# A stored order of steps, ScalarE's factors in registers and one fp32 head pair fewer, in attention followed by a gated MLP

## The chip, the core and the metric

The kernel runs on one core of a Trainium2 chip. The metric is the device time of one execution in microseconds, taken from the median of several runs. Five engines work side by side, each through its own instruction stream in order: TensorE (PE; PEld is its weight load), VectorE (DVE), ScalarE (ACT), GpSimd (POOL, nearly unused here) and SyncE (SP), which issues the DMAs. Engines wait for one another by semaphores.

## The reference

Attention with soft-capped scores over 4 batches of 12 heads (448 positions, 64 wide), then two matrix products with a gate between them:

```python
scores = cap * np.tanh(scale * np.matmul(q, k.transpose(0, 1, 3, 2)) / cap)
scores = scores - np.max(scores, axis=-1, keepdims=True)
attn = np.exp(scores)
attn = attn / (np.sum(attn, axis=-1, keepdims=True) + 1e-09)
x = np.matmul(attn, v)      # (4, 12, 448, 64), then laid out as (1792, 768)
h = x @ w_in                # 768 -> 2048
g = h * (1.0 / (1.0 + np.exp(-1.702 * h)))
out = g @ w_out             # 2048 -> 768
```

The two weights arrive as 64-bit floats.

## The kernel before

**Units.** Attention is cut into 24 units, one for each pair of heads: 6 pairs in each of 4 batches, in that order. Unit u makes the scores of its pair transposed (keys on the partitions) in four groups (`GROUPS`, three of two 448-column banks and one of one bank), and each group goes PE (tile `s`), Tanh on ACT (`t`), Exp on ACT, and then back to PE twice: `sm` sums the exponentials with a matrix of ones, `pa` multiplies them by v. DVE multiplies `pa` with the reciprocal of the sums (`rb`), which takes a way through four small DMAs (`sd`, `rsum`, `rd`, `rb`).

**Two kinds of unit.** The first `F32_UNITS` units (8 before) feed PE with fp32 operands, straight from the DMA: `kk`, `qh` and `vd` or space in `wo`. All later units are split: each fp32 tensor becomes a high and a low 16-bit float (`kk` with both halves stacked, `qh` and `ql`, `vh` and `vl`, `p` with two planes), and PE makes the products from those. For that a split unit needs one instruction that rounds each tensor, on ACT or DVE (`scaled`), and one that subtracts, on DVE (`stt`, `tt`).

**The MLP.** Batches 0 and 1 go through `h_unit` (6 x 3 matmuls into `m` for each of 16 rows of h) and `o_unit` (16 x 3 for each of 6 rows of the output). Batches 2 and 3 go together, by a seven-product scheme: `moe_sums` prepares sums of weight blocks, `x_last` sums of activations, `h_quad` makes eight sets of seven products into six banks `z`, and `seven_first` and `seven` the output. DVE decodes the 64-bit weights into two 16-bit halves (`decode_w`) in the meantime.

**PE's tile forms.** PE holds matmuls of five forms (rows x columns of the array): 128x128 for the MLP and the scores of split units, 64x128 and 64x64 for fp32 scores, 128x64 for `pa`, 128x32 for `sm`. I call a step from a matmul of one form to one of another a switch.

**The order.** Nothing runs when it is recorded. `Plan.op` keeps each step with its engines (some steps may go to ACT or DVE, `scaled`), its duration by a table and what it depends on. `schedule` then runs a list scheduler: 30 passes of `forward` (the step that can start first goes next, ties by priority) and `backward` (new priorities from the latest starts), keeps the best pass, and `refine` moves runs of PE steps of one form next to runs of the same form if that makes the modelled total shorter. Buffers of a ring get their slots in passing. `emit` writes the steps out in that order.

**ACT's factors.** Tanh takes its scale from `tsc`, Exp its scale from `capt` and, in split units, its bias from `lnb`: three 128x1 tiles, one number for each partition, read by every such instruction.

Of the kernel before, what the change touches and what calls it, by code (L numbers as in the profile page):

```python
# [9 lines left out]
F32 = mybir.dt.float32  # L10
# [13 lines left out]
F32_UNITS = 8  # L24
# [11 lines left out]
PASSES = 30  # L36
# [15 lines left out]
PE_TURN = 0.093  # L52
# [5 lines left out]
DVE_SHY = (1.0,)  # L58
STAY = (0.0,)
ROUNDS, RUN, REACH = 4, 6, 20.0  # L60
# [48 lines left out]
class Plan:  # L109
# [118 lines left out]
    def start_over(self):  # L228
        bufs = {b for o in self.ops for b in o.bufs}
        for b in bufs:  # L230
            b.left, b.freed = 0, 0.0
            if b.ring:
                b.slot = None
        for o in self.ops:
            o.left, o.ready = len(o.deps), 0.0
            o.eng = next(iter(o.ways)) if len(o.ways) == 1 else None
            for b in o.bufs:
                b.left += 1
        for r in self.rings:
            r["free"] = [(0.0, i) for i in range(len(r["tiles"]))]  # L240
            r["queue"] = list(r["turns"])

    def forward(self, shy, stay=0.0):

        self.start_over()
        free = {"PE": 0.0, "ACT": ACT_FROM, "DVE": ACT_FROM, "SP": 0.0}
        cand = {e: [o for o in self.ops if e in o.ways and not o.left] for e in free}
        turn, pipe = None, 0.0
        order = []
        while len(order) < len(self.ops):  # L250
            best = None
            for e, c in cand.items():
                for o in c:
                    t = max(o.ready + (shy if e == "DVE" and len(o.ways) > 1 else 0.0), free[e])
                    for b in o.bufs:
                        if b.slot is None:
                            r = b.ring
                            t = max(t, r["free"][0][0]) if r["free"] and (r["any"] or r["queue"][0] is b) else math.inf
                    k = (t, o.prio + (stay if e == "PE" and o.turn != turn else 0.0), o.ways[e][0])
                    if best is None or k < best[0]:  # L260
                        best = (k, e, o)
            assert best is not None and best[0][0] < math.inf, "no step can go on"
            (t, _, us), e, o = best
            for w in o.ways:
                cand[w].remove(o)
            o.eng, o.emit = e, o.ways[e][1]
            for b in o.bufs:
                if b.slot is None:
                    b.ring["queue"].remove(b)
                    b.slot = b.ring["free"].pop(0)[1]  # L270
            if e == "PE":
                us += PE_TURN * (o.turn != turn)
                turn = o.turn
            o.start, o.end = t, t + us
            free[e] = t + us
            done = t + us + LAG[e]
            if e == "SP":
                pipe = max(pipe, t + us) + o.mb / DMA_BW
                done = pipe + LAG[e]
            order.append(o)  # L280
            for u in o.users:
                u.left -= 1
                u.ready = max(u.ready, t + us if u.eng == e == "PE" else done + HANDOFF)
                if not u.left:
                    for w in u.ways:
                        cand[w].append(u)
            for b in o.bufs:
                b.left -= 1
                b.freed = max(b.freed, done + HANDOFF)
                if not b.left and b.ring:  # L290
                    b.ring["free"].append((b.freed, b.slot))
                    b.ring["free"].sort()
        return order

    def backward(self, order):

        after = {o: [(u, 0.0 if u.eng == o.eng == "PE" else LAG[o.eng] + HANDOFF) for u in o.users] for o in order}
        turns = {}
        for o in order:
            for b in o.bufs:  # L300
                if b.ring:
                    x = turns.setdefault((id(b.ring), b.slot), [])
                    if not x or x[-1][0] is not b:
                        x.append((b, []))
                    x[-1][1].append(o)
        for x in turns.values():
            for (_, was), (_, then) in zip(x, x[1:]):
                for o in was:
                    after[o].append((then[0], LAG[o.eng] + HANDOFF))
        before = {o: [] for o in order}  # L310
        for o, xs in after.items():
            for u, lag in xs:
                before[u].append((o, lag))
        left = {o: len(xs) for o, xs in after.items()}
        end = max(o.end for o in order)
        due = {o: end for o in order}
        free = dict.fromkeys(("PE", "ACT", "DVE", "SP"), end)
        cand = [o for o in order if not left[o]]
        start = {}
        while cand:  # L320
            o = max(cand, key=lambda o: (min(due[o], free[o.eng]), o.end))
            cand.remove(o)
            free[o.eng] = start[o] = min(due[o], free[o.eng]) - (o.end - o.start)
            for q, lag in before[o]:
                due[q] = min(due[q], start[o] - lag)
                left[q] -= 1
                if not left[q]:
                    cand.append(q)
        return start

    def schedule(self):

        best = None
        for i in range(PASSES):
            stay = STAY[i % len(STAY)] if i else 0.0
            order = self.forward(DVE_SHY[0], stay)
            total = max(o.end for o in order)
            if best is None or total < best[0]:
                best = (total, stay, {o: o.prio for o in order})
            for o, t in self.backward(order).items():  # L340
                o.prio = t
        for o, p in best[2].items():
            o.prio = p
        self.order = self.forward(DVE_SHY[0], best[1])
        self.refine(ROUNDS)
# [21 lines left out]
    def timed(self, pre, seqs, limit=math.inf):  # L367
# [5 lines left out]
        turn, pipe, left = None, 0.0, n  # L373
        while left:
            moved = False
            for e, s in seqs.items():
                k = at[e]
                while k < len(s):
                    i = s[k]
                    t = free[e]  # L380
                    for p, near in pre[i]:
                        if start[p] is None:
                            t = None
                            break
                        x = end[p] if near else done[p] + HANDOFF
                        if x > t:
                            t = x
                    if t is None:
                        break
                    o = self.order[i]  # L390
                    us = o.ways[e][0]
# [4 lines left out]
                    free[e] = t + us  # L396
                    if e == "SP":
                        pipe = max(pipe, t + us) + o.mb / DMA_BW
                        done[i] = pipe + LAG[e]
                    else:  # L400
                        done[i] = t + us + LAG[e]
                    if end[i] > limit:
                        return None
                    k += 1
                    left -= 1
                    moved = True
                at[e] = k
            if not moved:
                return None
        return start, end, max(end)  # L410

    def refine(self, rounds):

        pre = self.edges()
        seqs = {e: [i for i, o in enumerate(self.order) if o.eng == e] for e in ("PE", "ACT", "DVE", "SP")}
        start, end, best = self.timed(pre, seqs)
        for _ in range(rounds):
            gained = False
            k = 1
            while k < len(seqs["PE"]):  # L420
                s = seqs["PE"]
                turn = lambda j: self.order[s[j]].turn
                if turn(k) == turn(k - 1):
                    k += 1
                    continue
# [1130 lines left out]
```

## Time and profile before

| | |
|---|---|
| Time, median of 3 runs | 603.84 us (603.43 to 603.88) |
| The profiled execution | 603.16 us |
| Its span, first to last instruction | 600.9 us |
| Granted TensorE clock, mean | 0.998 |
| PE busy | 589.3 us, 98% of the span, 3666 matmuls |
| PE's weight loads busy | 281.5 us, 47% |
| DVE busy | 540.5 us, 90%, 898 instructions |
| ACT busy | 414.2 us, 69%, 610 instructions |
| DMA | 73.87 MB, 123 GB/s over the span |
| Chain that ended last | PE 86%, DVE 5%, DMA 4%, ACT 2% |

The span is the time between the first and the last instruction on the core; 2.26 us of the profiled execution lie outside it. Busy times are unions of an engine's instructions, so two that overlap by a little count once. The helper functions record every operation, so nearly all instructions carry one of a few line numbers (L218 is every matmul, L183 most of DVE, L175 and L199 most of ACT), and tile names tell them apart.

### The profile page before, as it was taken

The page shows a single profiled execution, that of the slowest core. Times are in us where ns is not written, and L with a number is a line of the kernel's source. Part 1 is how long each engine was busy: PE and PEld are TensorE (multiplying, and loading weights), DVE is VectorE, ACT ScalarE, POOL GpSimd, SP SyncE. Part 2 cuts the span into 40 slices and gives each one's busy share as a digit, 9 for nine tenths or more (in the row PEclk, how much of TensorE's full clock was granted, in tenths as well). Part 3 has the DMA queues.
Part 4 walks back from the last instruction along what each step waited for, and adds up shares of the span by engine and source line. Part 5 has one row for each costly group of instructions (what it writes and reads, how often), then busy time and mean ns, then how long its engine had stood idle before and what let it go on. Part 6 is the DMA issues. An engine that isn't in the chain of part 4 may idle for free.

```text
span 600.9 us, 9852 instructions
## 1 busy us (share of the span) xinstructions
PE 589.3 (98%) x3666; PEld 281.5 (47%) x3666; DVE 540.5 (90%) x898; ACT 414.2 (69%) x610; POOL 0.2 (0%) x4
## 2 busy tenths in 40 slices
PE   7999999999999999999999999999999999999995
PEld 3332344444544444445554445455555555555552
DVE  4999999999999999999999989878999999968912
ACT  5998896999987987999879779834555554211100
POOL 0000000000000000000000000000000000000000
PEclk9999999999999999999999999999999999999999
DMA  8988864226567443513343453022222210001001
GB/s 297 383 234 246 296 220 149 81 53 208 154 193 231 157 130 87 178 46 109 109 122 130 127 174 120 30 83 58 71 76 65 53 54 1 31 15 47 32 15 50
DMA packets 45556, 73.87 MB, mean 123 GB/s; under 512 B 14952, under 2 KB 31168, under 8 KB 45504
## 3 DMA queue, kind: packets, MB, share of 16 engines
q1 hardware_dynamic: 45504, 73.20, 38.4%
q8 instruction: 30, 0.49, 0.3%
q14 instruction: 22, 0.18, 0.1%
HBM read 61.22 MB, written 11.95 MB: 122 GB/s over the span
## 4 chain that ended last, share of the span: by engine, by line
PE 86%; DVE 5%; DMA 4%; ACT 2%; issue 1%; SPq 1%; DVEq 0%; ACTq 0%
PE m L218 43%; PE z L218 22%; PE s L218 9%; PE pa L218 9%; PE sm L218 3%; DMA wo<-in_moe_w_in_dram 1%; DMA rd<-rr 1%; ACT t L175 1%; SPq L224 1%; DVE ta L183 1%; DMA stg<-in_kx_dram 1%; DVE p L183 1%; ACT p L175 1%; DMA wo<-in_q_dram 1%; DVE f L183 0%
## 5 line engine op out<-in xcount | busy, mean ns | idle before, releaser
L218 PE MATMUL m<-g,wo 128*128 128x448 f16 x624 | 127.4, 353 | 0.0
L218 PEld LDWEIGHTS <-wo 128*128 128x128 f16 x864 | 81.8, 98 | 82.0 <-issue 9.0
L175 ACT ACTIVATE t<-s,tsc 128x896 f32<-128x896 f32 x96 | 86.8, 918 | 17.4 <-PE s L218 13.7
L218 PEld LDWEIGHTS <-wi_h 128*128 128x128 f16 x528 | 49.4, 98 | 56.2 <-issue 12.2
L218 PE MATMUL m<-x,wi_h 128*128 128x448 f16 x234 | 63.6, 353 | 0.0
L175 ACT ACTIVATE t<-t,lnb,capt 128x896 f32<-128x896 f32 (+1 forms) x58 | 59.4, 1030 | 0.4
L183 DVE TENSOR_TENSOR p<-t,p 128x896 f16<-128x896 f32 (+1 forms) x58 | 55.2, 954 | 4.1 <-ACT p L199 3.7
L218 PE MATMUL m<-xa,wi_h 128*128 128x448 f16 x198 | 53.7, 353 | 0.0
L218 PE MATMUL s<-qh,kk 128*128 128x448 f16 (+3 forms) x160 | 48.1, 403 | 0.0
L199 ACT ACTIVATE p<-t 128x896 f16<-128x896 f32 (+1 forms) x54 | 45.1, 838 | 0.3
L183 DVE SCALAR_TENSOR_TENSOR wo<-wo 128x1024 int32<-128x1024 int32 (+2 forms) x42 | 43.8, 1064 | 0.0
L218 PE MATMUL m<-x,wi_l 128*128 128x448 f16 x117 | 41.2, 352 | 0.0
L218 PEld LDWEIGHTS <-stg 128*128 128x128 f16 x288 | 28.2, 98 | 26.3
L218 PE MATMUL s<-ql,kk 128*128 128x448 f16 (+1 forms) x128 | 39.6, 352 | 0.0
L218 PEld LDWEIGHTS <-wi_l 128*128 128x128 f16 x264 | 25.8, 98 | 24.1
L199 ACT ACTIVATE xa<-x 128x1024 f16<-128x1024 f32 x9 | 9.5, 1057 | 38.3 <-PE z L218 27.3
L218 PE MATMUL pa<-p,vh 128*64 128x448 f16 x256 | 35.6, 356 | 0.4 <-DVE rb L183 0.4
L218 PE MATMUL m<-xa,wi_l 128*128 128x448 f16 x99 | 34.9, 352 | 0.0
L218 PEld LDWEIGHTS <-kk 128*128 128x128 f16 (+1 forms) x256 | 20.8, 100 | 23.4 <-issue 6.8
L218 PE MATMUL sm<-p,ones 128*32 128x224 f16 (+2 forms) x544 | 30.8, 313 | 0.5 <-ACT p L175 0.5
L218 PEld LDWEIGHTS <-xa 128*128 128x128 f16 x216 | 21.1, 98 | 19.6
L175 ACT ACTIVATE p<-t,capt 128x896 f32<-128x896 f32 (+1 forms) x32 | 29.6, 970 | 0.0
(282 smaller groups left out, 1078.4 us busy)
## 6 DMA issues: line engine op xcount, KB each, us to landing
wo<-in_moe_w_in_dram SPq DMA_DIRECT2D x18, 512.0 KB
stg<-in_kx_dram SPq DMA_DIRECT2D x16, 448.0 KB
stg<-in_qx_dram SPq DMA_DIRECT2D x16, 448.0 KB
stg<-in_moe_w_out_dram SPq DMA_DIRECT2D x16, 384.0 KB
wo<-in_moe_w_out_dram SPq DMA_DIRECT2D x16, 384.0 KB
sum<-xa SPq DMA_DIRECT2D x32, 192.0 KB
stg<-sum SPq DMA_DIRECT2D x32, 192.0 KB
rb<-rd SPq DMA_DIRECT2D x44, 112.0 KB
```

The source lines that it names most:

```text
L175: self.nc.scalar.activation(real(out), real(in_), func, scale=real(scale), **b)
L183: getattr(self.nc.vector, name)(out=real(out), **{k: real(x) for k, x in ins.items()}, **kw, **a)
L199: self.nc.scalar.activation(real(out), real(in_), AF.Copy, scale=1.0 if f is None else f, **b)
L218: self.nc.tensor.matmul(real(o), real(w), real(x), start=a, stop=z)
L224: self.nc.sync.dma_start(real(o), real(i))
```

## The change

There are three edits.

1. `F32_UNITS` is 7 instead of 8: unit 7 (batch 1, second pair) becomes a split unit.
2. `tsc` (two tiles) and `capt` are loaded into registers of ScalarE once, at the start (`held`, a register load on ACT), and Tanh and Exp name the register as their scale; Exp's bias is the constant log(64) in the instruction, and `lnb` is gone. None of these instructions reads a 128x1 tile any more. Since the planner's price of an ACT instruction depends on the number of such tiles, it now counts Tanh and Exp as cheaper.
3. The list scheduler (`start_over`, `forward`, `backward`, `refine`) is gone. `ORDER` is a compressed string: one 16-bit number for each step (the step's number, and one bit for which of its engines takes it), then one byte for each use of a ring for the slot. `schedule` reads it, and `timed` only gives the steps their places for `emit`.

```diff
-F32_UNITS = 8
+F32_UNITS = 7
...
+ORDER = (
+    "c-p;p1F+{!vSpSMzqW1Lwr$(C-F^SKecQHe+qP}nHeY`;`(|f1Uc`%;c)L|~PE}-NMpd1tjHpxqU_gTf1Of;7z2p!LQiBI6AUX)7fou>LQbGjC1u-Bkq=J}`6e2=)U`PiAy-1K7VnG?m0g)jORDjqJ1<FDk$O{!A"
...
     def schedule(self):
 
-        best = None
-        for i in range(PASSES):
...
-        self.order = self.forward(DVE_SHY[0], best[1])
-        self.refine(ROUNDS)
+        n = len(self.ops)
+        raw = zlib.decompress(base64.b85decode(ORDER))
+        slots = iter(raw[2 * n:])
         for r in self.rings:
+            for b in r["turns"]:
+                b.slot = next(slots)
+        self.order = []
+        for x in struct.unpack(f"<{n}H", raw[:2 * n]):
+            o = self.ops[x & 0x7FFF]
+            o.eng = list(o.ways)[x >> 15]
+            o.emit = o.ways[o.eng][1]
+            self.order.append(o)
...
+    def held(t):
+        r = nc.scalar.alloc_register()
+        nc.scalar.reg_load(r, t[:1].bitcast(I32))
+        return r
...
-        tsc.append(plan.fixed(t))
-    capt, lnb = plan.fixed(capt), plan.fixed(lnb)
+        tsc.append(held(t))
+    capt = held(capt)
...
-                plan.act(e[:, :nn], t[:, :nn], AF.Exp, scale=capt, bias=lnb)
+                plan.act(e[:, :nn], t[:, :nn], AF.Exp, scale=capt, bias=math.log(PS))
```

Counted over the whole order, PE switches its form 186 times before and 100 times now (the last check's one matmul left out); of these 80 and 52 have an fp32 matmul on one side.

PE, first fp32 units, from the first `pa` on (`s` are scores, `pa` products with v, `sm` sums; two instructions of one matmul count as x2). Before:

```order
L218 MATMUL pa_156<-p_134,wo 64x448 x2
L218 MATMUL sm_155<-p_134,ones_2_75 32x224 x4
L218 MATMUL sm_155<-p_135,ones_2_75 32x224 x4
L218 MATMUL s_160<-wo 128x448 x2
L218 MATMUL pa_156<-p_135,wo 64x448 x2
L218 MATMUL pa_156<-p_136,wo 64x448 x2
L218 MATMUL sm_155<-p_136,ones_2_75 32x224 x4
L218 MATMUL sm_155<-p_137,ones_0_73 32x224 x2
L218 MATMUL sm_155<-p_137,ones_1_74 32x224 x2
L218 MATMUL pa_156<-p_137,wo 64x448 x2
```

and now, in the same place:

```order
L257 MATMUL pa_161<-p_139,wo 64x448 x2
L257 MATMUL sm_160<-p_139,ones_2_74 32x224 x4
L257 MATMUL sm_160<-p_140,ones_2_74 32x224 x4
L257 MATMUL s_165<-wo 128x448 x2
L257 MATMUL s_166<-wo 128x448 x2
L257 MATMUL sm_160<-p_141,ones_2_74 32x224 x4
L257 MATMUL sm_160<-p_142,ones_0_72 32x224 x2
L257 MATMUL sm_160<-p_142,ones_1_73 32x224 x2
L257 MATMUL s_165<-wo 128x448 x2
L257 MATMUL s_166<-wo 64x448 x2
L257 MATMUL pa_161<-p_140,wo 64x448 x2
L257 MATMUL pa_161<-p_141,wo 64x448 x2
```

The three later `pa` of the first unit, which stood in two places, now stand together behind its sums, and scores of the next unit are drawn ahead of them.

ACT, its first steps after the table load (`t` is Tanh's output, `p` Exp's). Before:

```order
L529 ACTIVATE warm<-lnb 128x1
L175 ACTIVATE t_131<-s_160,tsc_111 128x896
L175 ACTIVATE t_132<-s_161,tsc_111 128x896
L175 ACTIVATE p_134<-t_131,capt 128x896
L175 ACTIVATE p_135<-t_132,capt 128x896
```

and now:

```order
L412 ACTIVATE warm<-warm 128x1
L432 TENSOR_LOAD tsc_110
L214 ACTIVATE t_136<-s_165 128x896
L214 ACTIVATE t_137<-s_166 128x896
L432 TENSOR_LOAD capt
L214 ACTIVATE p_139<-t_136 128x896
L214 ACTIVATE p_140<-t_137 128x896
```

One register load now stands ahead of the first Tanh, another between the second Tanh and the first Exp; the third stands ahead of the first split unit's Tanh.

SP, its first DMAs (`g` and `wo` are room for weight pieces, keys, queries and v that wait to be used). Before:

```order
L524 DMA capt<-in_cap_dram 128x1
L224 DMA wo<-in_k_dram 128x448
L224 DMA wo<-in_q_dram 128x448
L224 DMA wo<-in_v_dram 128x512
L224 DMA wo<-in_k_dram 128x448
L224 DMA wo<-in_q_dram 128x448
L224 DMA g<-in_moe_w_in_dram 128x1024 x4
```

and now:

```order
L408 DMA capt<-in_cap_dram 128x1
L263 DMA wo<-in_q_dram 128x448
L263 DMA wo<-in_k_dram 128x448
L263 DMA g<-in_moe_w_in_dram 128x1024 x2
L263 DMA wo<-in_v_dram 128x512
L263 DMA wo<-in_k_dram 128x448
L263 DMA wo<-in_q_dram 128x448
```

Two weight pieces moved ahead of v and of the second unit's keys and queries.

## Rows read from the trace of the kernel before

**Rows 1.** The page's part 1: busy time, share of the span, instructions.

```profile
PE 589.3 (98%) x3666; PEld 281.5 (47%) x3666; DVE 540.5 (90%) x898; ACT 414.2 (69%) x610; POOL 0.2 (0%) x4
```

**Rows 2.** Windows of the span: length, then busy us of each engine, clock, DMA.

```profile
0.00:20.00 20.00, 16.37 (x100) 6.65 (x100) 10.84 (x37) 13.98 (x18) 0.20 (x4) 1.00 0.89 328
...
200.00:280.00 80.00, 79.79 (x506) 39.22 (x504) 79.08 (x126) 69.20 (x99) 0.00 (x0) 1.00 0.39 120
...
340.00:400.00 60.00, 60.00 (x445) 28.73 (x443) 49.68 (x87) 44.97 (x67) 0.00 (x0) 1.00 0.36 113
400.00:520.00 120.00, 120.00 (x638) 62.00 (x635) 117.52 (x209) 60.61 (x108) 0.00 (x0) 1.00 0.17 51
```

**Rows 3.** Chain that ended last, in order of time: start us, us, what.

```profile
205.17 1.14 PE m L218 x6
206.82 2.39 PE pa L218 x24
209.21 1.24 PE m L218 x6
```

**Rows 4.** PE's instructions in time, fp32 units: start, us, operation, idle before.

```profile
28.23 0.97 PE L218 MATMUL pa<-p,wo 128*64 128x448 f32 x4
29.13 0.96 PE L218 MATMUL sm<-p,ones 128*32 128x224 f32 x16
30.03 1.77 PE L218 MATMUL s<-wo 64*128 64x448 f32 x8
31.73 0.96 PE L218 MATMUL sm<-p,ones 128*32 128x224 f32 x16
32.63 1.72 PE L218 MATMUL pa<-p,wo 128*64 128x448 f32 x8
34.28 1.92 PE L218 MATMUL s<-wo 64*64 64x448 f32 x8
```

**Rows 5.** The same at 16-bit forms.

```profile
205.00 1.30 PE L218 MATMUL m<-g,wo 128*128 128x448 f16 x6
206.23 0.59 PE L218 MATMUL sm<-ta,ones 128*32 128x224 f32 x8
```

**Rows 6.** The same, where PE waited.

```profile
5.15 4.08 PE L218 MATMUL s<-wo 64*128 64x448 f32 x12 [1.37 <-DMA wo<-in_q_dram]
9.58 0.97 PE L218 MATMUL s<-wo 64*64 64x448 f32 x4 [0.35 <-ACT t L175]
...
43.03 1.02 PE L218 MATMUL s<-wo 64*128 64x448 f32 x4 [0.80 <-ACT t L175]
...
276.66 0.57 PE L218 MATMUL pa<-p,vh 128*64 128x448 f16 x4 [0.21 <-DVE rb L183]
```

**Rows 7.** Groups by form, ACT: count, busy us, mean ns, idle before.

```profile
L175 ACT ACTIVATE f<-m 128x448 f32<-128x448 f32 x32 | 17.2, 541 | 3.3 <-PE m L218 3.3
L175 ACT ACTIVATE t<-s,tsc 128x448 f32<-128x448 f32 x24 | 15.3, 638 | 1.3 <-PE s L218 1.0 <-DVE ta L183 0.3
L175 ACT ACTIVATE t<-t,lnb,capt 128x448 f32<-128x448 f32 x16 | 12.2, 761 | 0.1
L175 ACT ACTIVATE stg<-stg 128x448 f32<-128x448 f32 x6 | 3.4, 575 | 2.6 <-DVE stg L183 2.6
```

**Rows 8.** DVE's instructions in time.

```profile
9.23 0.43 DVE L183 TENSOR_SCALAR g<-g 128x512 int32<-128x512 int32 x1 [5.00 <-DMA g<-in_moe_w_in_dram]
...
385.95 0.62 DVE L183 TENSOR_TENSOR rb<-x,rb 128x448 f32<-128x448 f16 x1
386.49 0.62 DVE L183 SCALAR_TENSOR_TENSOR xa<-ta,xa 128x448 f16<-128x448 f32 x1
...
595.30 0.13 DVE L1383 TENSOR_SCALAR flag<-cnt 1x1 int32<-1x1 f32 x1
```

**Rows 9.** SP's DMA issues in time.

```profile
2.14 0.43 SPq L224 DMA_DIRECT2D wo<-in_v_dram  x1
...
3.56 2.06 SPq L224 DMA_DIRECT2D g<-in_moe_w_in_dram  x4
```

More of the change, by code (lines that the diff above doesn't have):

```diff
@@ L1 @@
+import base64
 import math
+import struct
+import zlib
 from contextlib import ExitStack
@@ L243, in forward @@
[L243 to L250, printed above, removed]
-            best = None
[L252 to L329, printed above, removed]
@@ L331, in schedule @@
-    def schedule(self):
-        best = None
-        for i in range(PASSES):
[L335 to L343, printed above, removed]
-        self.order = self.forward(DVE_SHY[0], best[1])
-        self.refine(ROUNDS)
+    def schedule(self):
+        n = len(self.ops)
+        raw = zlib.decompress(base64.b85decode(ORDER))
+        slots = iter(raw[2 * n:])
+        for r in self.rings:
+            for b in r["turns"]:
[6 more added lines that the diff above has]
+            self.order.append(o)
+        seqs = {e: [i for i, o in enumerate(self.order) if o.eng == e] for e in LAG}
+        start, end, self.total = self.timed(self.edges(), seqs)
+        for i, o in enumerate(self.order):
+            o.start, o.end = start[i], end[i]
+        self.order = [self.order[i] for i in sorted(range(n), key=lambda i: (start[i], i))]
@@ L365, in edges, with timed @@
         return [list(dict(sorted(p)).items()) for p in pre]
[L367 removed]
+    def timed(self, pre, seqs):
         n = len(self.order)
@@ L372, in timed @@
         free = {"PE": 0.0, "ACT": ACT_FROM, "DVE": ACT_FROM, "SP": 0.0}
-        turn, pipe, left = None, 0.0, n
-        while left:
+        turn, pipe = None, 0.0
+        while any(at[e] < len(s) for e, s in seqs.items()):
             moved = False
             for e, s in seqs.items():
[L377 to L389, printed above, removed]
+                while at[e] < len(s) and all(start[p] is not None for p, _ in pre[s[at[e]]]):
+                    i = s[at[e]]
                     o = self.order[i]
+                    t = max([free[e]] + [end[p] if near else done[p] + HANDOFF for p, near in pre[i]])
                     us = o.ways[e][0]
@@ L395, in timed @@
                     start[i], end[i] = t, t + us
-                    free[e] = t + us
+                    free[e] = done[i] = t + us
                     if e == "SP":
[L398 to L405, printed above, removed]
+                        done[i] = pipe = max(pipe, t + us) + o.mb / DMA_BW
@@ L406, in timed @@
+                    done[i] += LAG[e]
+                    at[e] += 1
                     moved = True
[L407 to L409 removed]
+            assert moved, "no step can go on"
         return start, end, max(end)
[L412 to L425, printed above, removed]
[L426 to L449 removed]
@@ L524, in fast_path @@
     nc.sync.dma_start(capt, cap.to_broadcast([P, 1]))
-    lnb = sb.tile([P, 1], F32, name="lnb")
-    nc.vector.memset(lnb, math.log(PS))
     warm = sb.tile([P, 1], F32, name="warm")
-    nc.scalar.activation(warm, lnb, AF.Tanh)
+    nc.vector.memset(warm, 0.0)
+    nc.scalar.activation(warm, warm, AF.Tanh)
     ones32 = [sb.tile([P, D], F32, name=f"ones32_{i}") for i in range(3)]
```

78 lines of the change are left out of this document (37 added, 41 removed).

## The prediction

> **What bounds the kernel now.** I read the busy times first: PE is busy 98% of the span, DVE 90%, ACT 69% [rows 1]. A busy PE proves little, so I looked at its rate. In the chain that ended last, six full matmuls take 1.14 us, 0.19 us each, the same wherever they stand [rows 3], and the chain is PE's for 86%. Then I went through PE's instructions in time for places where it stood still. There are few: it starts its first scores at 5.15, whose twelve instructions need 4.43 us to the next row where 2.4 would do (PE waits for Tanh to empty the banks), and later it waits 0.80 us on ACT and 0.21 us on DVE [rows 6]; with smaller ones about 4 us after the start. So the time is PE's work, plus some 4 us of waits, plus a start and an end that the change leaves alone.
>
> DVE is close behind: in 200 to 280 us it works 79.08 of 80 us, in 400 to 520 117.52 of 120. It has room only in 340 to 400, where it idles 10.3 of 60 us [rows 2]. A shorter PE must not run into DVE; that is the main doubt.
>
> **The changed form order on PE.** The new order has 86 switches fewer. What one costs is in the rows: six matmuls of the MLP take 1.14 us in a run and 1.24 us with a switch [rows 3], and at the sums 1.23 us from 205.00 to 206.23 [rows 5]; 24 `pa` take 2.39 us [rows 3] where 12 x 0.19 = 2.27 would be their work. That is 0.10 to 0.12 us; I take 0.105. Among fp32 forms four `pa` take 0.90 us (28.23 to 29.13) and eight take 1.65 (32.63 to 34.28) [rows 4]: 0.75 for four and 0.15 for the switch. Of the 86, 28 touch fp32 matmuls and 58 do not: 28 x 0.15 + 58 x 0.105 = **10.3 us** less. All of it lies on PE, which is the path.
>
> **One fp32 pair fewer.** An fp32 pair has 16 score instructions (0.78 us for four, from eight in 1.70 us less a switch), 16 `pa` (0.75 for four) and 32 sums (0.75 for sixteen) [rows 4]: 3.1 + 3.0 + 1.5 = 7.6 us. A split pair has 12 full score matmuls (2.3 us), 4 narrow ones that run in twos (0.4), 24 `pa` (2.3) and sums worth four full matmuls (0.8) [rows 3]: 5.7 us. PE gains **1.9 us**. Together PE's work falls by 12.2 us.
>
> The split pair costs DVE five subtractions of 896 columns, one of 512 and one of 448. DVE's pitch at 448 columns is 0.54 us (385.95 to 386.49) [rows 8], so some 6 us. The new order also moves roundings from DVE to ACT (all 17 of `kk` are on ACT now, 11 of 16 before). Adding up all DVE instructions of both orders with such pitches gives DVE 3.7 us more work in all.
>
> **Factors in registers.** A Tanh of 448 columns from PSUM takes 541 ns with its scale in the instruction and 638 ns with `tsc`; an Exp with `capt` and `lnb` takes 761 ns where the same length without them takes 575 ns [rows 7]. So a tile of factors costs 97 ns, two cost 186. 96 Tanhs, 64 Exps with two and 32 with one: 9.3 + 11.9 + 3 = 24 us off ACT. The trace has no instruction with a register as scale. Its price lies between nothing (the row with the number in the instruction; a gain beyond that has no reason) and the tile's 97 ns; I take nothing, since no partition's factor is fetched any more. ACT hardly shows on the path, so the 24 us are worth little by themselves: they pay for the roundings it takes from DVE and shorten PE's waits in the first 60 us.
>
> Each of the three register loads happens once. No row shows one; at the program's end 5.5 us pass from the flag's write at 595.30 [rows 8] to the end of the span, which contain one load and much else, so a load costs between nothing and 5.5 us. The first is covered: ACT has nothing to do until PE has made scores. The second stands between the second Tanh and the first Exp and may hold up Exp once; I take nothing, and keep 1 to 3 us for the range. The Trainium skill (Runtime: NRT & Kernel Launch, "The ~15µs preamble/postamble breakdown") gives about 1.3 us for a register load from HBM; by that, an estimate, the sum would be up to 1.3 us higher, and no row here shows it.
>
> **What is late next: DVE.** For every wait of PE on DVE I added up the PE work ahead of the waiting matmul and the DVE work ahead of the instruction that it waits for. The difference is the margin by which DVE may lag behind PE. Before, the smallest margin is 6 us at 100 us of PE work, 9.8 at 260 to 290 and 33 at 420 to 480; now it is 4, 7.2 and 19.4. At 276.66 PE did wait for DVE, 0.21 us [rows 6], so there DVE's lag was the whole margin. The new margin is 2.6 us smaller. Against that, DVE starts sooner: its first weight piece came at 9.23 [rows 8], issued from 3.56 on behind five loads of 1152 KB; now it takes the place of the load issued at 2.14 [rows 9], behind 448 KB. 704 KB at the 328 GB/s of the first 20 us [rows 2] are 2.1 us (the two issues alone are 1.4 apart). So PE ends up waiting 0.5 us more than before, about 4.5 us in place of 4, now on DVE and not on ACT. In the last third the margin shrinks by 13.6 us, and what DVE has for it is the 2.1 us and the 10.3 us of idle time in 340 to 400, most of which was waiting for PE and goes when PE comes sooner.
>
> **The sum.** The profiled execution took 603.16 us: 603.16 - 10.3 - 1.9 + 0.5 = 591.5. The median of the runs is 0.7 above the profiled one, so I forecast **592.2 us**, 1.9% faster.
>
> **Rivals.**
>
> *PE waits for nobody.* If the shorter ACT instructions and the earlier start of DVE remove all waits, 4.5 us more go: 587.7. Against it stands DVE's full load [rows 2].
>
> *A register costs as much as a tile.* About 40 such ACT instructions stand ahead of PE's tightest wait in the first 60 us, where ACT's margin is 3.1 us (1.9 before). 40 x 0.097 = 3.9 us of delay, of which 1.2 are covered by the margin: 2.7 more, 594.9.
>
> *DVE stays behind in the last third.* If the idle 10.3 us in 340 to 400 [rows 2] are a latency (the four small DMAs behind the sums) and stay, PE is held up by up to 13.6 - 2.1 = 11.5 us, less what was spare before, which no row shows. I price it at half, 5.8 us: 598.0. For it: the last two units wait on that way in both orders. Against it: the new order puts 78 MLP matmuls, 14.9 us, between the last unit's sums and its `pa`.
>
> *The register stalls ACT.* If ACT had to empty before each instruction that names a register, the same 40 instructions would delay PE in the first 60 us. From 0.35 us each the 14 us eat PE's gain; at 0.4 us the delay is 16 - 1.2 = 14.8 us and the time 606.5, slower than before. Nothing in the trace speaks for so much.
>
> *DVE sets the time.* If the end follows DVE's work, which grows by 3.7 us, and DVE starts 2.1 us sooner, the time is 603.84 + 1.6 = 605.4. For it: DVE's full stretches [rows 2]. Against it: DVE idles 10.3 us in 340 to 400 while PE works all 60, and PE's wait for DVE in the rows is 0.21 us [rows 6]. The Trainium skill (Perfetto Trace Analysis, "Identifying the Most-Contended Engine") calls matmul busy time a bad measure and wants the busy share of weight loads; by that PE, at 47%, would not be the limit and DVE would, which is this rival. The unchanging 0.19 us for a matmul in rows 3 speaks against it here.
>
> **How the numbers follow.** The forecast (590 to 594) 0.56; no waits 0.10; a register as a tile 0.12; DVE behind in the last third 0.14; a stall on registers 0.03; DVE sets the time 0.03; no effect, since the saved switches come back as waits one for one, 0.02. The range holds the forecast, the tile's price and most of the two cases on either side: 587 to 598. About 0.2% is what a measurement of this kernel can tell from no change. Faster 0.92, same 0.02, slower 0.06.
>
> **What would show it.** PE's busy time should fall by about 12 us and the span with it. In the chain, runs of `m` and `pa` should be longer. Tanh of 448 columns should take 0.54 us and Exp 0.58 to 0.60; 0.64 and 0.67 would be the tile's price. DVE's first row should be near 7 us, and its idle time in the stretch that answers to 340 to 400 nearly gone. PE's waits on ACT in the first 60 us should shrink and small waits on DVE, 0.2 to 1 us each, appear between 100 and 390. The forecast is wrong if a switch costs PE nothing once the neighbours change, or if waits on DVE add up to more than 10 us.

## The result, and the profile of the changed kernel

| | before | changed |
|---|---|---|
| Time, median | 603.86 us (603.43 to 604.53, 4 runs) | 594.87 us (594.74 to 595.72, 4 runs) |
| The profiled execution, its span | 603.16, 600.9 us | 594.82, 592.7 us |
| First `z` matmul (batches 2 and 3 in the MLP) | 407.02 us | 397.51 us |
| From there to the end of the last matmul | 187.70 us | 187.70 us |
| From there to the end of the span | 6.2 us | 7.5 us |

The ratio is 0.9853 (95% interval 0.9836 to 0.987): 1.5% faster, 9.0 us where 11.6 were forecast. The time lies in the range, 2.7 us above the forecast. All of the gain comes ahead of the first `z`; the last 195 us give 1.3 back.

The lines that answer to [rows 1], busy time, share of the span, instructions:

```profile
PE 579.4 (98%) x3674; PEld 289.8 (49%) x3674; DVE 544.7 (92%) x904; ACT 399.4 (67%) x617; POOL 0.2 (0%) x4
```

PE is busy 9.9 us less, DVE 4.2 more, ACT 14.8 less. To [rows 2], windows (start and end, length, then busy us of PE, PEld, DVE, ACT, POOL, clock, DMA share, GB/s), moved up by 10 us where the program runs ahead:

```profile
20.00:60.00 40.00, 38.86 (x257) 13.82 (x258) 38.13 (x47) 38.94 (x53) 0.00 (x0) 1.00 0.93 292
200.00:280.00 80.00, 79.31 (x504) 40.17 (x503) 78.97 (x126) 71.90 (x108) 0.00 (x0) 1.00 0.44 136
330.00:390.00 60.00, 60.00 (x468) 31.48 (x465) 58.15 (x104) 38.82 (x62) 0.00 (x0) 1.00 0.42 129
390.00:510.00 120.00, 120.00 (x647) 61.96 (x646) 114.37 (x199) 54.87 (x105) 0.00 (x0) 1.00 0.19 57
```

DVE's 10.3 idle us of 340 to 400 are down to 1.9. ACT, whose instructions became shorter, is fuller than ever in 20 to 60 (37.39 us before). To [rows 3], the chain in order of time, where six `m` and a switch alternated:

```profile
126.93 2.84 PE m L257 x15
130.64 2.39 PE pa L257 x24
133.41 13.73 PE m L257 x72
```

These runs are longer, as forecast, but they are not the whole chain. At the time that answers to before's 205, it has left PE:

```profile
195.42 1.09 DVE p L222
197.90 5.20 DMA rsum<-sd
```

and its shares, from the page, are those of PE 66% where it was 86% and of DVE 16% where it was 5%:

```profile
PE 66%; DVE 16%; ACT 7%; DMA 5%; issue 4%; SPq 0%; ACTq 0%; DVEq 0%
```

A chain share is no price: the DVE links lead up to PE's waits below, and what they are worth is measured in e6_dve.

To [rows 6], PE's instructions in time with the idle time before them:

```profile
5.13 6.17 PE L257 MATMUL s<-wo 64*128 64x448 f32 x16 [1.35 <-DMA wo<-in_k_dram]
42.91 2.48 PE L257 MATMUL pa<-p,wo 128*64 128x448 f32 x12 [0.35 <-ACT pu L238]
48.20 1.02 PE L257 MATMUL s<-wo 64*128 64x448 f32 x4 [0.56 <-DMA rb<-rd]
213.63 0.57 PE L257 MATMUL pa<-p,vh 128*64 128x448 f16 x4 [0.41 <-DVE rb L222]
240.82 0.57 PE L257 MATMUL pa<-p,vh 128*64 128x448 f16 x4 [0.26 <-DVE rb L222]
289.68 0.57 PE L257 MATMUL pa<-p,vh 128*64 128x448 f16 x4 [0.28 <-DVE rb L222]
```

The first row is long without a wait. Its sixteen score matmuls need 3.3 us at the rate of the later ones and are listed with 6.17, and PE has no idle time inside the row. The groups of these matmuls say more (count, busy us, mean ns): in 5.5 to 8.2 us before, in 5.5 to 9.1 us now, and in 13.6 to 14.5 us now.

```profile
L218 PE MATMUL s<-wo 64*128 64x448 f32 x8 | 3.3, 980 | 1.4 <-DMA wo<-in_q_dram 1.4
L257 PE MATMUL s<-wo 64*128 64x448 f32 x12 | 4.8, 975 | 1.3 <-DMA wo<-in_k_dram 1.3
L257 PE MATMUL s<-wo 64*128 64x448 f32 x8 | 1.8, 562 | 0.0
```

Pairs of them start 0.75 us apart in the first row and 0.37 to 0.38 us apart later. The trace's record of the granted clock begins, at 1.00, only at 10.80 us (8.32 before), and at just that time the matmuls change from one pace to the other: two of one form that start at 9.91 and 10.71 take 1.00 and 0.58 us. So until then PE works at half pace in both kernels, that of the lower of the clock's two levels, 1.2 in place of 2.4 GHz; the windows print 1.00 for this stretch since no record covers it. ACT waits for PE there, and not PE for ACT:

```profile
8.53 0.92 ACT L214 ACTIVATE t<-s 128x896 f32<-128x896 f32 x1 [0.58 <-PE s L257]
```

To count waits I took for each row the time to the start of the next, less its matmuls at their full rate, less 0.10 us where the form changes. Gaps over 0.15 us add up to 4.7 us before and 7.6 us now: 5.0 of these 7.6 lie in the first 70 us (3.9 before) and 2.5 between there and the first `z` (0.7 before). The half pace at the start is part of them: from 5.15 to 8.32 it costs 1.6 us before, from 5.13 to 10.80 2.8 us now. What is left of waits in the first 70 us is 2.3 us before and 2.2 us now.

To [rows 7], ACT by form (count, busy us, mean ns, idle before):

```profile
L214 ACT ACTIVATE f<-m 128x448 f32<-128x448 f32 x32 | 17.1, 542 | 2.0 <-PE m L257 1.8 <-PE pa L257 0.2
L214 ACT ACTIVATE t<-s 128x448 f32<-128x448 f32 x24 | 13.1, 546 | 7.8 <-DVE p L222 6.2 <-DVE rr L222 1.4
L214 ACT ACTIVATE t<-t 128x448 f32<-128x448 f32 x17 | 9.7, 572 | 0.2
```

A scale in a register costs what a scale in the instruction costs: 546 against 542 ns for Tanh (638 with the tile), 572 for Exp (761 with two tiles). To [rows 8, 9], DVE's first two rows of the weights and SP's issues:

```profile
8.23 0.43 DVE L222 TENSOR_SCALAR g<-g 128x512 int32<-128x512 int32 x1 [4.03 <-DMA g<-in_moe_w_in_dram]
9.53 0.43 DVE L222 TENSOR_SCALAR g<-g 128x512 int32<-128x512 int32 x1 [0.86 <-DMA g<-in_moe_w_in_dram]
```

```profile
2.14 0.91 SPq L263 DMA_DIRECT2D g<-in_moe_w_in_dram  x2
3.09 0.43 SPq L263 DMA_DIRECT2D wo<-in_v_dram  x1
```

DVE starts 1.0 us sooner, not 2.1, and stands still again for 0.86 us until the second piece is there.

### The profile page after: what moved, and what is told of

It reads as the page before. It is cut to its first block, busy times and chain, and to the rows that moved or that the text cites. A ratio compares the mean times of both kernels' runs of the same rounds, so it can differ in the third digit from the quotient of the medians.

```text
span 592.7 us, 9836 instructions
## 1 busy us (share of the span) xinstructions
PE 579.4 (98%) x3674; PEld 289.8 (49%) x3674; DVE 544.7 (92%) x904; ACT 399.4 (67%) x617; POOL 0.2 (0%) x4
## 4 chain that ended last, share of the span: by engine, by line
PE 66%; DVE 16%; ACT 7%; DMA 5%; issue 4%; SPq 0%; ACTq 0%; DVEq 0%
PE m L257 32%; PE z L257 22%; PE s L257 5%; PE pa L257 5%; DVE wo L222 3%; ACT t L214 3%; DVE p L222 2%; PE sm L257 2%; DVE ta L222 1%; DVE g L222 1%; DVE f L222 1%; DVE ql L222 1%; DMA sd<-f 1%; DMA stg<-in_moe_w_out_dram 1%; ACT wo L238 1%
## 5 line engine op out<-in xcount | busy, mean ns | idle before, releaser
L257 PEld LDWEIGHTS <-wo 128*128 128x128 f16 x864 | 83.5, 98 | 80.5 <-issue 3.6
L214 ACT ACTIVATE t<-s 128x896 f32<-128x896 f32 (+1 forms) x96 | 77.8, 829 | 25.2 <-DVE p L222 14.4
L222 DVE TENSOR_TENSOR p<-t,p 128x896 f16<-128x896 f32 (+1 forms) x62 | 58.7, 954 | 0.3
L214 ACT ACTIVATE t<-t 128x896 f32<-128x896 f32 (+1 forms) x62 | 51.9, 846 | 0.6
L257 PE MATMUL s<-qh,kk 128*128 128x448 f16 (+3 forms) x152 | 46.0, 377 | 0.0
L257 PE MATMUL s<-ql,kk 128*128 128x448 f16 (+1 forms) x136 | 42.1, 352 | 0.0
L257 PE MATMUL pa<-p,vh 128*64 128x448 f16 x272 | 37.8, 355 | 0.9 <-DVE rb L222 0.9
L257 PEld LDWEIGHTS <-kk 128*128 128x128 f16 (+1 forms) x272 | 23.4, 101 | 22.5 <-issue 2.7
L257 PE MATMUL s<-wo 64*128 64x448 f32 (+1 forms) x96 | 25.1, 631 | 2.1 <-DMA wo<-in_k_dram 1.3
L257 PE MATMUL sm<-p,ones 128*32 128x224 f16 (+2 forms) x544 | 26.4, 305 | 0.0
```

The source lines that it names most:

```text
L214: self.nc.scalar.activation(real(out), real(in_), func, scale=real(scale), **b)
L222: getattr(self.nc.vector, name)(out=real(out), **{k: real(x) for k, x in ins.items()}, **kw, **a)
L257: self.nc.tensor.matmul(real(o), real(w), real(x), start=a, stop=z)
```

## The experiments

| run | what it is | median us (before in the same session) | ratio to before, 95% interval |
|---|---|---|---|
| e1_units | before, 7 fp32 pairs | 608.44 (605.23) | 1.0054 [1.0034, 1.0075] |
| e2_regs | before, registers | 608.34 (605.23) | 1.0068 [1.0044, 1.0091] |
| e3_both | before, both, list scheduler | 607.84 (605.23) | 1.0041 [1.0025, 1.0057] |
| e12_same_order | before's order, registers | 603.44 (604.43) | 0.9983 [0.9967, 0.9998] |
| e4_tiles | changed, factors as tiles | 600.97 (605.23) | 0.9930 [0.9906, 0.9953] |
| e5_switches | changed, 74 switches more | 600.30 (605.14) | 0.9914 [0.9887, 0.9940] |
| e6_dve | changed, DVE relieved | 590.64 (605.14) | 0.9754 [0.9729, 0.9779] |
| e7_tail | changed, last outputs on two queues | 593.92 (605.14) | 0.9807 [0.9782, 0.9833] |
| e8_v_first | changed, v ahead of the weights | 594.80 (605.14) | 0.9838 [0.9797, 0.9880] |
| e9_loads | changed, 15 register loads more | 595.35 (604.11) | 0.9848 [0.9819, 0.9876] |
| e10_ends | changed, e7 and cap's DMA moved | 595.60 (604.11) | 0.9850 [0.9822, 0.9879] |
| e11_again | changed, once more | 594.14 (604.11) | 0.9830 [0.9804, 0.9855] |

The changed kernel and its relatives share their order, so three landmarks of PE split their profiled executions (start of the first 128x128 `s` of a split unit, start of the first `z`, end of the last matmul). The `z` stage takes 187.70 us in each.

| | to first split `s` | from there to first `z` | last matmul to end of span |
|---|---|---|---|
| changed | 70.47 | 327.04 | 7.5 |
| e11_again | 72.39 | 326.71 | 6.1 |
| e7_tail | 72.58 | 326.60 | 5.2 |
| e8_v_first | 71.63 | 327.45 | 6.0 |
| e9_loads | 72.78 | 327.14 | 6.1 |
| e10_ends | 73.24 | 327.19 | 5.4 |
| e4_tiles | 73.21 | 331.67 | 6.5 |
| e5_switches | 71.28 | 333.60 | 5.9 |
| e6_dve | 71.96 | 324.17 | 6.2 |

The first column moves by over 2 us among executions whose programs hardly differ there, the third by over 1; the second stays within 0.9 for the first six. So I read effects from the second column.

### The edits without the table

```diff
-F32_UNITS = 8
+F32_UNITS = 7
```

> The kernel before with seven fp32 pairs and nothing else; the list scheduler orders it anew (184 switches of form in place of 196, counted with the ten of the slow path; 73 of them touch fp32 matmuls in place of 90). Theory, PE's work sets the time: 1.9 us less for the unit, 17 x 0.15 - 5 x 0.105 = 2.0 us less for the switches, so 600.0 us against 603.86. Rival, DVE sets the time: its work grows by 6 us, so about 609.9.

```diff
...
-        tsc.append(plan.fixed(t))
-    capt, lnb = plan.fixed(capt), plan.fixed(lnb)
+        tsc.append(held(t))
+    capt = held(capt)
...
-                plan.act(e[:, :nn], t[:, :nn], AF.Exp, scale=capt, bias=lnb)
+                plan.act(e[:, :nn], t[:, :nn], AF.Exp, scale=capt, bias=math.log(PS))
```

> The kernel before with ScalarE's factors in registers and nothing else; the list scheduler orders it anew (191 switches in place of 196). Theory, a register costs what the number in the instruction costs and ACT is off the path: ACT's work falls by 24 us, the switches are worth 12 x 0.105 - 7 x 0.15 = 0.2 us, and PE's waits on ACT in the first 60 us shrink by 0 to 2 us: 601.7 to 603.7. Rival, the register costs as much as the tile: ACT's work stays and the time is 603.7. Rival, the register stalls ACT by 0.4 us: about 618.

Both together:

> Both edits, seven fp32 pairs and registers, with the list scheduler and no stored table (189 switches in place of 196, 110 in the changed kernel). Theory, PE's work sets the time: 1.9 us for the unit, 13 x 0.15 - 6 x 0.105 = 1.3 us for the switches, 0 to 2 us of waits: 598.7 to 600.7; the stored table is then worth the remaining 4 to 6 us of the 9.0. Rival, the table is worth little and the registers and the unit make the gain: about 595 to 596.

All three came out slower than the kernel before, by 0.4 to 0.7%, against the theory; of the rivals only the 609.9 of e1_units comes near. Its trace has three waits of PE on ACT between 66 and 74 us (0.77, 0.85 and 0.95 us) and 1.7 us lost to the clock behind them (below), 4.3 us of the 7.3 by which its span is longer than before's; what made ACT late and where the rest goes isn't shown, so that rival's reason, DVE's work, isn't excluded there. In e2_regs the registers do what they should, yet the planner, given cheaper ACT steps, draws another order. Its page's first part, and that of e12_same_order, which has the registers in the order of before:

```profile
PE 589.9 (97%) x3669; PEld 283.6 (47%) x3669; DVE 536.8 (89%) x888; ACT 404.6 (67%) x620; POOL 0.2 (0%) x4
```

```profile
PE 589.5 (98%) x3666; PEld 281.5 (47%) x3666; DVE 540.2 (90%) x898; ACT 395.2 (66%) x610; POOL 0.2 (0%) x4
```

The second was made to separate the registers from that order. The planner there keeps the tiles' prices:

```diff
-        refs = isinstance(scale, Ref) + isinstance(bias, Ref)
+        refs = (not isinstance(scale, float)) + (bias != 0.0)
...
```

> The kernel before with the factors in registers, as e2_regs, but the planner goes on pricing Tanh and Exp as if they read the tiles, so that every engine keeps exactly the order of the kernel before (186 switches). Theory, what made e2_regs slower is the new order that the planner draws from cheaper ACT steps, not the registers: here ACT does 24 us less work in the same order, PE's waits on ACT in the first 60 us (0.87, 0.61 and part of 1.77 us) shrink, and the time is 1 to 3 us below the kernel before. Rival, the registers themselves slow the program: 3 to 4 us above it, as e2_regs. Rival, ACT is off the path in this order: the same time.

In the order of before the registers gain 1.0 us (0.1 to 2.0), the lower end of what was expected: ACT falls by 19.0 us of busy time and hardly any of it lay on the path. So e2_regs lost its 3 to 4 us to the order, not to the registers. e3_both is the changed kernel without the table: 1.0041 against 0.9853 and 0.9830 make 11 to 13 us, more than the whole gain. It has 79 switches more, and one more loss, its windows around a wait of PE (columns as above; the granted clock stands behind POOL's count):

```profile
64.00:66.00 2.00, 1.65 (x8) 0.47 (x6) 1.56 (x2) 0.53 (x1) 0.00 (x0) 1.00 1.02 349
66.00:68.00 2.00, 0.26 (x2) 0.26 (x4) 2.00 (x3) 1.69 (x3) 0.00 (x0) 0.88 0.63 250
68.00:70.00 2.00, 2.00 (x6) 0.54 (x8) 1.94 (x4) 1.94 (x4) 0.00 (x0) 0.50 0.69 169
70.00:72.00 2.00, 2.00 (x10) 0.51 (x8) 2.00 (x2) 1.97 (x3) 0.00 (x0) 0.76 0.95 379
```

### The table without the registers

```diff
-        tsc.append(held(t))
-    capt = held(capt)
+        tsc.append(plan.fixed(t))
+    capt, lnb = plan.fixed(capt), plan.fixed(lnb)
...
-                plan.act(e[:, :nn], t[:, :nn], AF.Exp, scale=capt, bias=math.log(PS))
+                plan.act(e[:, :nn], t[:, :nn], AF.Exp, scale=capt, bias=lnb)
```

> The changed kernel with its table, but with the factors as 128x1 tiles again (tsc, capt, lnb) in the same order of steps on every engine. ACT's work grows by some 24 us. Theory: in the first 60 us ACT has 3.1 us of margin and 40 instructions cost 0.097 us more each, 3.9 us, of which up to 2.7 come through: 594.9 + 2.7 = 597.6, and no more than 600. Rival, ACT is off the path everywhere and the registers are worth nothing in this order: 594.9. Rival, ACT's full work counts, since it is over 90% busy up to 120 us and 90% up to 280: 600 to 610.

600.97 us, or 599.6 set against the 603.86 of the first session: the registers are worth 0.8 to 1.0% in this order, 4.6 to 6 us, twice the 2.7 of the theory. That is at the border between the theory's limit of 600 and the rival in which ACT's full work counts (600 to 610); most of ACT's 21 us more (420.6 us busy against 399.4) don't come through. The place is not where the theory put it. The first 73.2 us are within the spread of the others, and 4.6 us are lost between 70 and 400 (331.67 against a mean of 327.02). There, in 200 to 280:

```profile
200.00:280.00 80.00, 78.95 (x498) 40.03 (x498) 78.64 (x124) 77.27 (x109) 0.00 (x0) 1.00 0.48 144
```

ACT is at 77 of 80 us, beside a DVE at 79 and a PE at 79: all three engines are full. Of PE's waits after 70 us two end with ACT's Tanh (0.36 us at 218.10, 0.33 at 279.20) and the others with DVE.

### The price of a switch

The table stays; 37 neighbours on PE change places:

```diff
...
+        pe = [i for i, o in enumerate(self.order) if o.eng == "PE"]
+        for k in SWAP:
+            i, j = pe[k], pe[k + 1]
+            self.order[i], self.order[j] = self.order[j], self.order[i]
```

> The changed kernel with 37 pairs of neighbouring steps on PE exchanged between 100 and 385 us, each at a border between two forms of 16-bit matmuls: the same instructions, 74 switches of form more (122 in place of 48), nothing moved by more than one step. Theory, a switch costs PE 0.105 us and PE is the path: 74 x 0.105 = 7.8 us more, less what PE's present waits on DVE in that stretch (about 2 us) absorb, so 600.6 to 602.6. Rival, PE has room there because DVE sets the pace from 60 to 330: less than 3 us more, under 598. Rival, a switch costs nothing: 594.9.

600.30 us, 0.3 below the theory's range and 2.3 above the rival's. The stretch to the first `z` is 6.6 us longer than the mean 327.02, while PE's gaps after 70 us shrink from 2.5 to 0.9: 8.2 us for 74 switches, 0.11 each. PE's busy time says the same:

```profile
PE 585.7 (98%) x3674; PEld 282.7 (47%) x3674; DVE 546.4 (91%) x904; ACT 400.2 (67%) x617; POOL 0.2 (0%) x4
```

It is 6.3 us higher for the same instructions. A PE that DVE paced could not have lost these 6 us.

### What DVE holds up

```diff
-                plan.tt(pb[:, 1, :nn], t[:, :nn], pb[:, 0, :nn], ALU.subtract)
+                low, src = pb[:, 1, :nn], pb[:, 0, :nn]
+                plan.op({"DVE": (0.3, lambda low=low: nc.vector.memset(real(low), 0.0))}, [low], [t[:, :nn], src])
```

> The changed kernel with DVE relieved: the low part of the exponentials in split units is set to zero by a memset in place of the subtraction t - p (so those products lose their low part). 68 instructions of 0.96 us become short ones, DVE's work falls by some 40 us, the order stays. Theory, PE's work sets the time and DVE only adds the small waits seen between 60 and 330 (about 2 to 3 us): 592 to 593. Rival, DVE sets the pace of the first 400 us: the time falls until PE's own work with no waits is left, 587 to 589. Rival, DVE costs nothing: 594.9.

```profile
200.00:280.00 80.00, 80.00 (x512) 39.78 (x511) 70.33 (x128) 72.03 (x109) 0.00 (x0) 1.00 0.46 138
```

DVE has 9.7 us of room there and PE works all 80. The stretch is 324.17 us, 2.9 less than the mean, and no gap over 0.15 us is left in it. The chain is PE's again:

```profile
PE 88%; DMA 4%; DVE 3%; ACT 2%; issue 1%; SPq 0%; DVEq 0%; ACTq 0%
```

So what DVE holds up in this stretch of the changed kernel is 2.9 us, as the theory had it. The whole time is less clear: the median, 590.64, is 1.4 us below the theory's lower end and 3.5 to 4.2 us below the changed kernel's medians, and the ratios to before, 0.9754 against 0.9853 and 0.9830, make 4.6 to 6 us. Set against the 603.86 of the first session it is 589.0, the upper end of the rival's 587 to 589. The profiled execution, at 592.16, was the slowest of the four; what the faster ones gained outside this stretch has no trace.

### The two ends

```diff
-                self.nc.sync.dma_start(real(o), real(i))
+                (self.nc.scalar if x in self.late else self.nc.sync).dma_start(real(o), real(i))
...
+        self.late = {self.order[i] for i in seqs["SP"][-3::2]}
```

> The changed kernel with two of its last four output DMAs (second and fourth) issued from ACT, which has nothing left to do there, in place of SP. In the changed kernel SP issues those four one after the other in the last 5 us, the third taking 2.11 us, so that the last is issued at 588.02 although its data is ready at 585.87. Theory, the queue of issues on SP is what makes the end longer: the last issue comes at 586 and the time falls by 1.3 to 2.1 us, 592.8 to 593.6. Rival, the transfers themselves are the limit at the end: 594.9.

SP's last issues, in the changed kernel's first profile and then in e11_again, which is the same program:

```profile
584.97 0.80 SPq L263 DMA_DIRECT2D out_dram<-f  x1
585.81 2.11 SPq L263 DMA_DIRECT2D out_dram<-rb  x1
588.02 0.96 SPq L263 DMA_DIRECT2D out_dram<-f  x1
```

```profile
587.40 1.17 SPq L263 DMA_DIRECT2D out_dram<-rb  x1
588.68 0.68 SPq L263 DMA_DIRECT2D out_dram<-f  x1
```

The queue of issues is real, but its 2.11 us are a chance of one execution: 1.17 in the other, with 6.1 us from the last matmul to the end against 7.5. With two queues it is 5.2. So the edit is worth about 0.9 us of the usual 6.1, and the medians don't separate it from the changed kernel (0.9807 against 0.9830 and 0.9853, intervals overlapping).

```diff
+        a, b, c = sp[2:5]
+        self.order[a], self.order[b], self.order[c] = self.order[c], self.order[a], self.order[b]
```

> The changed kernel with v's first DMA ahead of the two weight pieces on SP's queue again, as before the change. Theory, PE's first pa at 11.23 waits for v, whose DMA stands behind 1 MB of weights: it starts at 10.4 to 10.6 and PE gains 0.7 us; DVE starts 0.5 to 0.8 us later (8.8 to 9.0 in place of 8.23) and gives back part of it as waits later: 594.2 to 594.9. Rival, pa waits for ACT's Exp: nothing changes at 11.23, and DVE's later start makes the time 594.9 to 595.7.

The first `pa` starts at 10.82. In the relatives with v behind the weights and the same start of PE it begins anywhere from 10.60 to 11.23, so neither theory holds: v's place doesn't move it. What it follows is the clock. In the nine profiled executions of this order the clock's record begins, at full, between 9.36 and 11.35 us, and the first `pa` comes the later, the later that is (10.60 in e5_switches, 11.63 in e10_ends). With PE's time ahead of the record counted at half, the way from the first score matmul to the first `pa` is 3.26 to 3.32 us in all nine, and PE has no idle time on it. DVE's first row moves to 8.70 and the time doesn't change (0.9838).

```diff
...
-    nc.sync.dma_start(capt, cap.to_broadcast([P, 1]))
+    nc.scalar.dma_start(capt, cap.to_broadcast([P, 1]))
```

> The changed kernel with the two edits at its ends: two of the last four outputs issued from ACT (as in e7_tail), and capt's DMA issued from ACT at the start, so that SP issues the first queries at 0.75 in place of 1.20. Theory, PE starts 0.45 us sooner and the end is 1 to 2 us shorter: 592.5 to 593.5 where the changed kernel has 594.9, and 0.4 less than e7_tail. Rival, the first transfers are limited by the DMA engines and not by SP's issue: as e7_tail, 593.0 to 593.9.

```profile
0.75 0.40 SPq L263 DMA_DIRECT2D wo<-in_q_dram  x1
1.20 0.43 SPq L263 DMA_DIRECT2D wo<-in_k_dram  x1
```

```profile
5.40 6.31 PE L257 MATMUL s<-wo 64*128 64x448 f32 x16 [1.62 <-DMA wo<-in_k_dram]
```

The queries and keys are issued 0.45 us sooner and PE starts at 5.40, not sooner than 5.13. The rival holds for the start; the time shows no gain at all. The Trainium skill (DMA: Bandwidth & Descriptors, "Issuing engines are not separate DMA queues") says that DMAs of all issuers run on the same 16 engines and that a second issuer saves only the time of issuing; by that rule little was to be had, and this start agrees.

### Register loads

```diff
-    capt = held(capt)
+    caps = [held(capt) for _ in range(16)]
...
-                plan.act(e[:, :nn], t[:, :nn], AF.Exp, scale=capt, bias=math.log(PS))
+                plan.act(e[:, :nn], t[:, :nn], AF.Exp, scale=caps[min(u, 15)], bias=math.log(PS))
...
-                plan.act(pp[:, :nn], t[:, :nn], AF.Exp, scale=capt)
+                plan.act(pp[:, :nn], t[:, :nn], AF.Exp, scale=caps[min(u, 15)])
```

> The changed kernel with capt loaded into 16 registers in place of one, each used by one unit's Exp, so that 15 more register loads stand on ACT, each ahead of the first Exp of its unit (six of them in the first 70 us, where ACT works nearly all the time). Theory, a register load costs nothing that shows: 594.9, and in the trace the Exp follows ACT's previous instruction at once. Rival by the bound of the forecast, 1 to 3 us each: 6 to 18 us in the first 70 us alone, 601 to 613. A price p in between shows as a gap of p ahead of each unit's first Exp.

ACT in time, first e9_loads, where a load stands between the two instructions, then the changed kernel, where none does:

```profile
23.23 0.61 ACT L238 ACTIVATE pu<-pa 128x448 f32<-128x448 f32 x1
23.65 1.03 ACT L214 ACTIVATE p<-t 128x896 f32<-128x896 f32 x1
```

```profile
23.37 0.61 ACT L238 ACTIVATE pu<-pa 128x448 f32<-128x448 f32 x1
23.79 1.02 ACT L214 ACTIVATE p<-t 128x896 f32<-128x896 f32 x1
```

0.42 us from start to start in both: the load costs ACT nothing. It runs from 22.47 to 22.75, while ACT is still at an earlier instruction (one that started at 21.91). All sixteen loads of `capt`, with their shortest, median and longest time in ns:

```profile
L432 ACTq TENSOR_LOAD <-capt x16: 276/280/710, 8.6 to 239.3; - x16
```

The ratio is that of the changed kernel within the intervals.

### The changed kernel once more

> The changed kernel as it is, on the chip of these runs, to set the others against. All theories: 594.9 to 596. The time until the first split scores (70.5 us in its first profile, 71.3 to 73.2 in the experiments) and the end after the last matmul (7.5 us there, 5.9 to 6.4 in experiments that leave the end alone) show how far these two move from one execution to the next.

594.14 us. Its first 72 us were 1.9 us longer than in the first profile and its end 1.3 shorter.

## Why the prediction was right, and what it mis-sized

**PE bounds the kernel: right.** e5_switches makes PE's work longer and the time follows; e6_dve takes a tenth of DVE's work between 70 and 400 us away and gains 2.9 of 327 us in that stretch. One ground given for it, PE's share of the chain, says little: it fell from 86 to 66%, while 2.9 us hung on DVE in that stretch.

**The switch term, 10.3 us: the 16-bit part shown, the rest consistent.** 0.11 measured for the 0.105 taken. The 0.15 for fp32 forms and the unit's 1.9 us were not run by themselves (e1_units changes the order too). They rest on the balance: 12.2 us less work and 2.9 us more in gaps make 9.3, and the first `z` comes 9.5 us sooner (7.9 in e11_again, the same program, whose first stretch is 1.9 us longer). So the balance can't tell these two terms, 4.2 and 1.9 us, from others of 1 or 2 us. That PE's busy time fell by 9.9 and not by 12.2 is no contradiction, since the half pace at the start counts as busy.

**PE's waits, +0.5 us: mis-sized, and this is the main miss.** The gaps grew by 2.9 us. First, the step read the start wrongly: the 4.43 us for twelve matmuls were put down to PE waiting for Tanh to empty the banks, but nearly all of the excess, except the 0.35 us listed at 9.58, is PE at half pace. That costs 1.6 us in the profile before and 2.8 in the one now, 1.2 us that the sum didn't have; whether the change has a part in the later rise of the clock, or chance alone, isn't shown (9.65 in e12_same_order, 9.36 to 11.35 in the changed order). Second, DVE was to start 2.1 us sooner; it was 1.0: I divided the bytes ahead of its first piece by a mean rate, and the piece came 1.1 us later than that gives. Third, PE's waits on ACT in the first 60 us were to shrink; the table spends part of what ACT saves on roundings (19.0 us saved in the order of before, 14.8 here), ACT stays full (38.94 of 40 us in 20 to 60), and the waits there stayed at 2.2 us. Fourth, and most, the waits on DVE from 70 to 400 rose from 0.7 to 2.5 us (2.9 by e6_dve), although DVE's extra work was forecast well (3.7, found 4.2): I took the smallest margin and one wait at it, while the rows show a new wait at 213, at 240 and at 289.

**The end, left alone: wrong by 1.3 us in the one execution,** and right in the next: 7.5, then 6.1 against 6.2 us. With it the profiled sum closes: 603.16 - 9.5 + 1.3 - 0.1 (outside the span) = 594.9, found 594.82. In the forecast's terms it is 603.16 - 12.2 + 1.2 (clock) + 1.8 (waits on DVE) + 1.3 (end) - 0.1 = 595.2. The 0.7 us by which the median was to lie above the profiled execution were 0.05, which hides part of the miss: the profiled sum is off by 3.3 us, the median by 2.7.

**Registers: price right, worth wrong.** 0.546 and 0.572 us were forecast as 0.54 and 0.58, and the loads cost nothing. The Trainium skill's figure (Runtime: NRT & Kernel Launch, "The ~15µs preamble/postamble breakdown"), 1.3 us, is for register loads from HBM, and no run here shows one. The loads of this kernel read SBUF, take 0.28 us each (median of sixteen) and hold nothing up. But "worth little by themselves" holds only in the order of before, 1.0 us. Under the table it is 4.6 to 6 us, twice what the rival of the tile's price reckoned, because that rival looked at the first 60 us alone, and ACT is at 77 of 80 us later on. I should have set the 24 us against ACT's new load stage by stage, as I did for DVE. These 4.6 to 6 us are no further term of the sum: they are waits that this order would have without the registers.

**The rivals.** DVE staying behind in the last third: no. DVE is busy 58.15 of 60 us in 330 to 390 and PE has no gap over 0.1 us from 292 to the first `z`. PE waiting for nobody, ACT stalling on registers, and DVE setting the time (605.4) all fall with the rows above. The rival of the tile's price gave 594.9, the measured time to 0.1 us, and is wrong all the same: Tanh takes 546 ns and not 638, so the agreement is chance. Of the signs named in advance, three did not come true: DVE's first row (8.23, not 7), the waits on ACT, and PE's busy time, which fell by 9.9 us and not by about 12.

What stays open: why the clock rises when it does, the price of a switch between fp32 forms and the worth of the unit by themselves, and whether e7_tail's version is faster than the changed kernel.

## What to carry to other kernels

Where three engines are full at once, edits are worth what the order lets them be: the same registers gained 1 us in one order and 5 in another, and a planner given them lost 3 to 4, so an edit is to be measured at a fixed order and with the order that was made for it. A shorter bound engine uses up margins of the next ones one after the other: count waits stage by stage for each engine that is over 90% busy, and take the sum of busy time for work only where like matmuls start at the same distance everywhere. A row that is too long need not hide a wait: compare the mean time of its instructions with that of later ones first, since PE at the lower clock looks just like it. One profile is not enough to place 1 us at the start or the end of a program; a stretch in between, from one landmark to another, held to 0.9 us in six executions.

## What the runs showed of the hardware beyond that

A register as the scale of an ACT instruction costs within 4 ns of a number in the instruction, and its load from SBUF costs ACT nothing that shows, even sixteen times.

After PE had stood still for 2.1 us ahead of 67.74, having worked 1.65 and 0.26 us of two stretches of 2 us, the granted clock fell from 1.00 to 0.50 in e3_both (2.4 to 1.2 GHz). For some 3.5 us PE got 0.88, 0.50 and 0.76 of its clock in windows of 2 us, 1.7 us lost in all. e1_units had 0.50 in 74 to 76, after PE had idled 0.8 to 0.95 us in three of the four stretches of 2 us from 66 on. So that wait cost nearly twice its length.

At the start, PE had worked from 1.92 to 3.8 us, stood still until the first keys came at 5.13, and then worked at half pace until 10.80 us in the changed kernel's profile (8.32 before, 9.36 to 11.35 in the experiments on the changed order), with 0.98 us for a matmul that takes 0.56 later. That costs 1.6 to 3.0 us of each execution, and nothing on the page tells of it, since the granted clock is printed as 1.00 there.

An SP that issues four outputs of 224 KB in a row was held up for 1.17 to 2.11 us at the third, where the first takes 0.34.
